# Two cached-attention blocks on one core: the wait for a pack's output weights moves to GpSimd, and the flag copy moves behind the last sum

## The chip, the core and the metric

The kernel runs on one core of a Trainium2 chip. A core has five instruction streams that run beside each other: TensorE (PE, matmuls; PEld is its weight load), VectorE (DVE), ScalarE (ACT), GpSimd (POOL) and SyncE (SP, which here only issues DMA transfers). Streams wait for each other through semaphores. The metric is the device time of one launch in microseconds (us); less is better.

## The reference

There are two independent blocks, A and B, of the same form; their results stand side by side in the output.

```python
# x [16, 64, 640], k_cache and v_cache [16, 32, 512, 128], wq [640, 4096], wo [4096, 640], all bf16
q = (x @ wq) -> [16, 32, 64, 128]
scores = einsum("bhqd,bhkd->bhqk", q, k_cache) * 128 ** -0.5
p = softmax(scores)
o = einsum("bhqk,bhkd->bhqd", p, v_cache)
return o -> [16, 64, 4096] @ wo
```

Nearly all bytes are the K and V caches: 2 blocks x 2 caches x 16 x 32 x 512 x 128 bf16 values.

## The kernel before, in words

**Packs.** The work is cut into 128 packs. A pack is four heads of a pair of batch rows, so its 2 x 64 queries fill 128 partitions. Four packs in a row (j = 0 to 3) make a group: 16 heads of one batch pair. Eight groups make a phase: one block and one half of its heads. There are four phases of 32 packs: A first half, A second half, B first half, B second half.

**What a pack does.** For pack n, in the names of the code and with the lines under which the profile shows them: QP (L684, PE) projects the queries, QE (L690, ACT) copies them out; KT (L698, DVE, two instructions) transposes the loaded K; S (L708, PE) makes the scores; EX (L737, ACT, four instructions, one for each head) takes the exponential and its sum; RC (L750, DVE, two instructions) inverts the sums; NM (L758, POOL, four instructions, heads 4n to 4n+3) multiplies P by them; TR (L770, PE) transposes P; TE (L850, DVE, two instructions, b = 0 and 1) copies transposed P out of PSUM; PV (L863, PE) multiplies by V; OE and ZO (L871, L875, ACT) copy the result out and clear PSUM; OP (L883, PE) multiplies by the pack's rows of wo and adds up over the four packs of a group in PSUM; OS (L893, L896, DVE) takes the sum out at the end of a group. At the start of a group XT, XE, XS and XC (L658, L664, L673) turn x around, and around the start of a phase WP (L652, POOL) lays out the next query weights.

**Loads.** SP issues all loads from one list: V (L642, L644; four pack slots), K (L631; six pack slots), x (L605), wq (L613) and wo (LDWO, L621). wo has four slots, one for each j, of 640 KB each. A slot is loaded once in a phase, for the phase's first group, and read by eight packs. In the list the load of wo for pack n stands behind V of pack n and K of pack n+3, and ahead of V of pack n+1. V of pack n waits until TR of pack n-3 is done.

**The order.** A planner (`build_plan`) gives every operation a due time, in packs, from the table `AT`: due time = pack + offset. Each engine's program is its operations sorted by due time, and each engine runs its program strictly in that order. From what operations read and write the planner finds which must wait for which, leaves out what an engine already knows through an earlier wait, and writes the rest as semaphore waits. For pack n the due times are: TE n+1.432 and n+1.47, PV n+1.701, OP n+2.387; NM of the next pack n+1.803 to n+2.187; TR of the next pack n+2.293. So between TE of pack n and OP of pack n, PE does PV of pack n, S of pack n+2 and TR of pack n+1, and TR of pack n+1 waits for the last NM of pack n+1.

**Where a wait may stand.** OP reads the wo slot, but does not wait for its load itself: a loop behind the planner's dependencies moves that wait to another operation that comes earlier and that PE waits for anyway. It moves two sorts: LDWO (the loads) and WZ (the clearing of two slots that two empty packs -2 and -1 read). The same loop puts the wait for a load of x (LDX) on the last NM of a pack, on POOL.

**The end.** The last pack (127) is done in two halves. OSH (L835, DVE, two instructions, due 127+1.75 and 127+1.8) adds each half of the last sum into the output tile, and SP stores each half (STH, L842, 80 KB). The kernel also checks that no sum left a safe range: FL1 (L908 to L915, DVE), FLM (L919, PE) and FLC (L923, DVE, due 127+1.77) leave a flag in SBUF. Each of the five streams waits for FLC, loads the flag into a register (L987) and branches (L988) over a second version of the program, which runs only where the flag says so. SP then waits for the stores (L529).

Of the kernel before, what the change touches and what calls it, by code (L numbers as in the profile page):

```python
# [20 lines left out]
class Cfg:  # L21
# [16 lines left out]
              RCZ=(0.475, 0.6), NMZ=(0.48, 0.49, 0.61, 0.62), TR=1.293, TE=(1.432, 1.47), PV=1.701, OE=(1.888, 2.013), ZO=2.221,  # L38
              OP=2.387, OS=2.576, LDWO=2.6, ST=2.8,
              TRH=(1.0, 1.05), TEH=(1.15, 1.2), TEX=1.2, PVH=(1.45, 1.46), OEH=(1.5, 1.55), OPY=(1.1, 1.57),  # L40
              OPZ=(1.65, 1.7), OSH=(1.75, 1.8), STH=(1.85, 1.9), FL1=1.3, FLM=1.68, FLC=1.77, WP0=-1.75,
              WP1=(-3.5, -2.55, -2.45, -1.5, -0.5, 0.5, 0.6, 1.5))


# [42 lines left out]
def build_plan(dims, cfg, general):  # L87
# [6 lines left out]
    N = NPH * PH  # L94
# [3 lines left out]
    at = {}  # L98

    def add(eng, kind, idx, ts, reads=(), writes=()):  # L100
        op = Op(eng, kind, idx, ts, reads, writes)
        ops.append(op)
        at[(kind, idx)] = op
        return op

    def add_output(n):
# [6 lines left out]
        if n == N - 1:  # L113
            for a in range(2):
# [5 lines left out]
                    [("B", 4), ("B", 5), ("xe", 0)] if a == 0 else [("SB", 2), ("SB", 3), ("xe", 1)])  # L120
                add("pe", "OPH", (n, a), n + AT["OPZ"][a], [("xe", 0), ("xe", 1), ("wo", j)], [("B", 6 + a)])
                add("dve", "OSH", (g, a), n + AT["OSH"][a], [("acc", g % NBP)], [("B", 6 + a), ("out_sb", a)])
# [47 lines left out]
    for ph in range(NPH):  # L170
        twp = [ph * PH + (AT["WP1"][i] if ph else i // 2 + AT["WP0"] + i % 2 * 0.001) for i in range(2 * NJ)]
        for kt in range(dims["KT"] if ph else 0):
            ready = twp[-1] - PH + 0.5 if ph > 1 else NJ - 1 + AT["WP0"] + 0.5
            op = add("sp", "LDWQ", (ph, kt), twp[0] - 0.5, [], [("ws", kt, j) for j in range(NJ)])
# [18 lines left out]
    for n in range(-2, N):  # L193
# [6 lines left out]
        for i in range(4):  # L200
            if i < 2 or n < cfg.KSPLIT:
                op = add("sp", "LDK", (n, i), n + AT["KT"][0] - 0.9, [], [("kn", n % cfg.NK)])
# [51 lines left out]

    for op in ops:
        if op.kind in ("OP", "OPH"):
            at[("TE", (op.idx, 1)) if op.kind == "OP" else ("TE", (op.idx[0], 1)) if op.idx[0] < N - 1 else ("TEH", 1)].deps += [d for d in op.deps if d.kind in ("LDWO", "WZ")]
            op.deps = [d for d in op.deps if d.kind not in ("LDWO", "WZ")]
        if op.kind == "XT" and op.idx > 0:
            at[("NM", 4 * (NJ * op.idx - NJ) + 3)].deps += [d for d in op.deps if d.kind == "LDX"]  # L260
            op.deps = [d for d in op.deps if d.kind != "LDX"]
        if op.kind == "QP" and op.idx > 0:
            op.deps = [d for d in op.deps if d.kind != "WP"]
# [238 lines left out]
def mha_kernel(nc, blocks, out, cfg=None):  # L502
# [20 lines left out]
    for general in (False, True):  # L523
        dims = dict(NPH=NPH, NBP=NBP, NJ=NJ, KT=KT, FIRST=lambda ph: ph % NSUB == 0,
                    FINAL=lambda ph: ph % NSUB == NSUB - 1)
        plans.append(build_plan(dims, cfg, general))
# [540 lines left out]
```

## Time and profile before

| | before |
|---|---|
| median of 3 runs | 738.27 us (737.86 to 738.68) |
| profiled execution, its own time | 737.86 us |
| span in that profile | 736.1 us |
| PE busy | 679.2 us (92%) |
| DVE / ACT / POOL busy | 526.9 / 533.2 / 416.5 us |
| read from HBM / rate over the span | 292.03 MB / 400 GB/s |

The span runs from the first to the last instruction of the program; the profiled execution's own time is 1.76 us longer. "Idle before, releaser" names what ended an engine's idle time. In the table of windows, DMA share is the summed time of packets over 16 engines' time, so it can be a little over 1. A landing time is the time from a transfer's issue until its semaphore says that it is done. "Chain" is the path followed back from the last instruction through whatever released each step.

### The profile page before, as it was taken

Reading aid. Unit: us, or ns where it says so; the run is one execution under the profiler, and the core shown is the slowest. Engines: PE = TensorE matmul, PEld = TensorE weight load, DVE = VectorE, ACT = ScalarE, POOL = GpSimd, SP = SyncE. Lnnn points to the kernel's source line nnn. Section 1 sums busy time; section 2 is a strip of 40 time slices with the busy share of each in tenths; the row PEclk is TensorE's granted clock in tenths of the full one; section 3 lists DMA queues with packets and bytes.
Section 4 is the critical chain, followed back from the end, with each engine's and each line's share of the span. In section 5 each row is a group of like instructions: output and inputs, shape, how many; then the busy total and the mean of one; then the engine's idle time right before and its main releaser. Section 6 shows DMA issues by size and latency. Waiting matters only on the chain.

```text
span 736.1 us, 61429 instructions
## 1 busy us (share of the span) xinstructions
PE 679.2 (92%) x28502; PEld 532.5 (72%) x28502; DVE 526.9 (72%) x819; ACT 533.2 (72%) x1574; POOL 416.5 (57%) x596
## 2 busy tenths in 40 slices
PE   3679999999989999999988999999998899999997
PEld 2457877877767777777766787777776678778785
DVE  7347877878767876867756777776676578788884
ACT  1348787877876887777865777777776687878874
POOL 3635656557864555454865565565577456555561
PEclk9889999999999999999998999999999999999999
DMA  8999999999999999999999999999999999999991
GB/s 325 393 392 411 415 415 414 414 416 413 416 400 410 417 417 416 415 419 416 416 412 400 416 414 414 414 414 413 416 416 405 404 418 417 415 419 416 417 400 45
DMA packets 76131, 295.06 MB, mean 401 GB/s; under 512 B 9536, under 2 KB 24512, under 8 KB 59712
## 3 DMA queue, kind: packets, MB, share of 16 engines
q1 hardware_dynamic: 73328, 291.90, 98.4%
q10 hardware_dynamic: 2768, 2.79, 1.2%
q8 instruction: 10, 0.16, 0.1%
q14 instruction: 25, 0.20, 0.1%
HBM read 292.03 MB, written 2.62 MB: 400 GB/s over the span
## 4 chain that ended last, share of the span: by engine, by line
PE 60%; DMA 27%; SPq 5%; DVE 3%; issue 2%; POOL 1%; ACT 0%; ACTq 0%
PE ps L863 14%; PE ps L883 13%; PE ps L684 12%; PE ps L708 12%; DMA wo_sb<-in_B_wo_dram 8%; PE ps L770 7%; DMA kn_ring<-in_B_k_cache_dram 5%; DMA kn_ring<-in_A_k_cache_dram 5%; DMA xn_ring<-in_B_x_dram 5%; SPq L631 3%; SPq L642 2%; DMA ws_sb<-in_A_wq_dram 2%; DMA wo_sb<-in_A_wo_dram 2%; DVE kt_ring L698 1%; DVE pT_sb L850 1%
## 5 line engine op out<-in xcount | busy, mean ns | idle before, releaser
L758 POOL TENSOR_SCALAR pn_ring<-pn_ring,recip 128x512 bf16<-128x512 bf16 x508 | 342.1, 692 | 244.9 <-DVE recip L750 238.5
L698 DVE STREAM_TRANSPOSE kt_ring<-kn_ring 128x1024 f32<-128x1024 f32 x256 | 302.4, 1220 | 65.9 <-DMA kn_ring<-in_B_k_cache_dram 35.7
L737 ACT ACTIVATE pn_ring<-ps 128x512 bf16<-128x512 f32 x512 | 296.4, 592 | 6.8 <-PE ps L708 6.8
L850 DVE COPY pT_sb<-ps 128x1024 bf16<-128x1024 bf16 x256 | 170.3, 676 | 103.5 <-PE ps L770 80.1
L863 PE MATMUL ps<-pT_sb,v_ring 32*128 32x64 bf16 x16448 | 162.1, 193 | 25.3 <-DVE pT_sb L850 12.7
L863 PEld LDWEIGHTS ps<-pT_sb,v_ring 32*128 32x128 bf16 x16448 | 147.5, 92 | 39.2 <-issue 28.7
L684 PE MATMUL ps<-xT_ring,wqp_sb 128*128 128x128 bf16 x2560 | 166.3, 221 | 7.5 <-POOL xT_ring L673 7.5
L684 PEld LDWEIGHTS ps<-xT_ring,wqp_sb 128*128 128x128 bf16 x2560 | 158.0, 114 | 14.0 <-issue 7.8
L883 PE MATMUL ps<-wo_sb,oT_sb 128*128 128x320 bf16 x1024 | 165.3, 305 | 0.0
L871 ACT ACTIVATE oT_sb<-ps 128x256 bf16<-128x256 f32 x257 | 84.7, 381 | 109.3 <-PE ps L863 109.3
L708 PE MATMUL ps<-kt_ring,qs_ring 32*64 32x512 bf16 x4096 | 140.6, 386 | 3.6 <-issue 3.6
L690 ACT ACTIVATE qs_ring<-ps 128x512 bf16<-128x512 f32 x128 | 76.4, 597 | 65.3 <-PE ps L684 62.6
L883 PEld LDWEIGHTS ps<-wo_sb,oT_sb 128*128 128x128 bf16 x1024 | 91.0, 99 | 37.9
L770 PEld LDWEIGHTS ps<-ident,pn_ring 64*128 64x128 bf16 x4096 | 68.8, 96 | 66.9 <-ACT oT_sb L871 48.0
L737 ACT ACTIVATION_READ_ACCUMULATOR pn_ring<-ps 128x1 f32 x512 | 105.3, 206 | 0.0
L770 PE MATMUL ps<-ident,pn_ring 64*128 64x64 bf16 x4096 | 83.8, 192 | 12.3 <-POOL pn_ring L758 4.5
L708 PEld LDWEIGHTS ps<-kt_ring,qs_ring 32*64 32x64 bf16 x4096 | 53.2, 104 | 33.2 <-issue 5.9
L750 DVE RECIPROCAL recip<-rowsum 128x2 f32<-128x2 f32 x256 | 41.0, 160 | 30.3 <-ACT pn_ring L737 24.6
L875 ACT ACTIVATE ps<-zeros 128x256 f32<-128x256 bf16 x128 | 49.5, 387 | 4.1
L652 POOL COPY wqp_sb<-ws_sb 128x1280 bf16<-128x1280 bf16 x32 | 39.5, 1253 | 18.3 <-DMA ws_sb<-in_A_wq_dram 15.1
L664 ACT ACTIVATE xe_sb<-ps 128x640 bf16<-128x640 bf16 x32 | 23.0, 717 | 3.6 <-PE ps L658 3.6
L673 POOL COPY xT_ring<-xe_sb 128x640 bf16<-128x640 bf16 x16 | 11.5, 716 | 21.9 <-PE ps L770 21.9
(42 smaller groups left out, 103.7 us busy)
## 6 DMA issues: line engine op xcount, KB each, us to landing
v_ring<-in_A_v_cache_dram SPq DMA_DIRECT2D x128, 512.0 KB, 12.9
kn_ring<-in_B_k_cache_dram SPq DMA_DIRECT2D x128, 512.0 KB, 14.0
v_ring<-in_B_v_cache_dram SPq DMA_DIRECT2D x128, 512.0 KB, 12.8
kn_ring<-in_A_k_cache_dram SPq DMA_DIRECT2D x112, 512.0 KB, 14.1
kn_ring<-in_A_k_cache_dram SPq DMA_DIRECT2D x32, 256.0 KB, 9.0
wo_sb<-in_A_wo_dram SPq DMA_DIRECT2D x8, 640.0 KB, 14.6
ws_sb<-in_B_wq_dram SPq DMA_DIRECT2D x10, 512.0 KB, 17.3
wo_sb<-in_B_wo_dram SPq DMA_DIRECT2D x8, 640.0 KB, 15.0
```

What stands on the lines that cost most here:

```text
L684: last = e.matmul(ps[:, 1, f * 128:(f + 1) * 128], w[:, kt, f, :], xT_ring[:, xs, kt, :], start=(kt == 0), stop=(kt == KT - 1))
L690: ins = e.activation(qs_ring[:, op.idx % NQ].rearrange("p f b q -> p (f b q)"), ps[:, 1, :], ACTF.Copy, scale=scale)
L698: ins = e.transpose(dst.rearrange("p c b (h l) -> p c h b l", h=8, l=2), src)
L708: last = e.matmul(ps[64 * b:64 * b + 64, i, :], qs_ring[rows, n % NQ, f, b, :], kt_ring[rows, n % NKT, :, f // 2, b, :, f % 2], start=(f = ...
L737: ins = e.activation(dst, src, ACTF.Exp, scale=1.0, accum_out=sum_of(h))
L758: ins = e.tensor_scalar(pn_view(h), pn_view(h), recip[:, h:h + 1], 1.0, ALU.mult, ALU.mult)
L770: last = e.transpose(pt_bank(b)[:, 64 * c:64 * c + 64], pn[rows, c, :], ident[rows, rows], tile_position=(64 * b, 0))
L850: ins = e.tensor_copy(pT_sb[:, b].rearrange("p t q -> p (t q)"), pt_bank(b))
L863: last = e.matmul(ps[:, 4 + i, 64 * b:64 * b + 64], v_ring[rows, n % NV, b, c, :], pT_sb[rows, b, c, :], start=(t == 0 and i < 2), stop=(t ...
L871: ins = e.activation(oT_sb[:, 2 * a:2 * a + 2, :], o_ps[:, 2 * a:2 * a + 2, :], ACTF.Copy)
L875: ins = e.activation(z_ps, zeros[:, :].unsqueeze(2).broadcast_to([128, 2, 128]), ACTF.Copy)
L883: last = e.matmul(out_ps[:, s, :], oT_sb[:, i, :], wo_sb[:, 4 * j + i, s * NH0:(s + 1) * NH0], start=(j == 0 and i == 0), stop=(j == NJ - ...
```

## The change

The wait for a load of wo (and for WZ) moves from the second TE of the same pack, on DVE, to the last NM of the next pack, on POOL: for OP of pack n that is NM of head 4n+7 (for the empty pack -2 it is NM -1, a clearing of a P slot). OP of the last two packs keeps its place (TE of pack 126, TEH of pack 127). The due time of FLC goes from 1.77 to 1.82, so that it stands behind both OSH on DVE instead of between them. No operation is added or removed.

```diff
-              OPZ=(1.65, 1.7), OSH=(1.75, 1.8), STH=(1.85, 1.9), FL1=1.3, FLM=1.68, FLC=1.77, WP0=-1.75,
+              OPZ=(1.65, 1.7), OSH=(1.75, 1.8), STH=(1.85, 1.9), FL1=1.3, FLM=1.68, FLC=1.82, WP0=-1.75,
...
     for op in ops:
         if op.kind in ("OP", "OPH"):
-            at[("TE", (op.idx, 1)) if op.kind == "OP" else ("TE", (op.idx[0], 1)) if op.idx[0] < N - 1 else ("TEH", 1)].deps += [d for d in op.deps if d.kind in ("LDWO", "WZ")]
+            at[("NM", 4 * op.idx + 7 if op.idx >= -1 else -1) if op.kind == "OP" else ("TE", (N - 2, 1)) if op.idx[0] < N - 1 else ("TEH", 1)].deps += [d for d in op.deps if d.kind in ("LDWO", "WZ")]
             op.deps = [d for d in op.deps if d.kind not in ("LDWO", "WZ")]
```

## The prediction

> **What bounds the kernel now.** I read the page first, which has PE busy for most of the span and the DMA engines busy in every slice but the first and the last; then busy time by 10 us windows, the waits, the timeline around a phase start and around the end, and last the chain. Four of the windows (the columns are the stretch and its length, PE, PEld, DVE, ACT and POOL busy, the granted clock, the DMA share and GB/s):
>
> ```profile
> 560.00:570.00 10.00, 6.69 (x315) 5.55 (x301) 6.20 (x9) 4.81 (x14) 5.28 (x8) 0.90 1.04 401
> 580.00:590.00 10.00, 7.04 (x380) 5.53 (x380) 6.67 (x10) 4.96 (x15) 4.07 (x6) 1.00 1.03 410
> 590.00:600.00 10.00, 10.00 (x447) 8.08 (x439) 8.12 (x14) 8.22 (x26) 5.38 (x8) 1.00 1.02 416
> 700.00:710.00 10.00, 10.00 (x440) 7.81 (x438) 7.83 (x12) 7.75 (x25) 5.88 (x10) 1.00 1.02 418
> ```
>
> Two limits lie almost on each other. The DMA engines are never idle while loads run: the DMA share stays above 1.00 and the rate near 416 GB/s, lower only where wo is loaded (401 to 410 at 560 to 590). PE, too, is full from 590 to the end. It idles at the phase starts, where four packs need 640 KB of wo each on top of their K and V. The waits on the tile of wo, its landing times, and two rows of the waits on POOL:
>
> ```profile
>   DVE pT_sb L850: 23.4, 12
> DMA to landing us min/median/max: 11.1/14.7/17.7
> ...
> POOL pn_ring L758 <- DMA xn_ring<-in_B_x_dram: 6.0, 6, 1.7
> PE ps L770 <- POOL pn_ring L758: 4.5, 6, 1.3
> ```
>
> TE (L850) waits for wo 12 times, four at each of three phase starts, 23.4 us in all. wo takes 11 to 18 us to land, with a full DMA queue ahead of it.
>
> **The change, part by part.** *1. The wait at a phase start.* The last phase starts at pack 96. The first, third and last of its four stalled copies, what follows the last on PE, and NM at the usual pace:
>
> ```profile
> 566.61 0.69 DVE L850 COPY pT_sb<-ps 128x1024 bf16<-128x1024 bf16 x1 [3.54 <-DMA wo_sb<-in_B_wo_dram]
> ...
> 580.35 0.69 DVE L850 COPY pT_sb<-ps 128x1024 bf16<-128x1024 bf16 x1 [2.01 <-DMA wo_sb<-in_B_wo_dram]
> ...
> 587.22 0.69 DVE L850 COPY pT_sb<-ps 128x1024 bf16<-128x1024 bf16 x1 [2.28 <-DMA wo_sb<-in_B_wo_dram]
> ...
> 588.05 1.21 PE L863 MATMUL ps<-pT_sb,v_ring 32*128 32x64 bf16 x128 [1.77 <-DVE pT_sb L850]
> ...
> 590.20 0.64 PE L770 MATMUL ps<-ident,pn_ring 64*128 64x64 bf16 x32
> ...
> 699.42 2.69 POOL L758 TENSOR_SCALAR pn_ring<-pn_ring,recip 128x512 bf16<-128x512 bf16 x4 [2.04 <-DVE recip L750]
> ```
>
> Today wo of pack 99 lands at 587.22; the copy, PV and S follow, and TR of pack 100 starts at 590.20, 2.98 us after the landing. With the wait on the last NM, copy, PV and S of pack 99 are done before the landing, and behind it stands one NM (four take 2.69 us, so 0.67 each) with about 0.1 us of semaphore: TR of pack 100 at 588.0. That is 2.2 us earlier. The same holds at the packs before it: each of the four transposes starts a landing plus 0.8, the first at 567.4 (566.61 + 0.8).
>
> What stands behind the waiting NM on POOL is NM of the next pack (its sums are not there yet), and once in a group XC; WP of the phase is all ahead of it. XC waits for the transpose just before it and takes as long as an OP, behind which PE comes to the QP that needs it: hidden, but with little to spare. On PE everything behind TR waits, but the first of it is OP, which needs that wo anyway. POOL's wait passes on almost whole: the waits for x that already stand on the same NM cost POOL 6.0 us and PE 4.5. Taking the wait off TE costs nothing; it only lets RC and KT, queued behind it on DVE, go earlier. SP issues the same list, and V of a later pack is let go by an earlier TR, so its issues come earlier or as now.
>
> *2. What is late next.* The landings stay where they are, since the DMA engines were never idle: an earlier issue only waits longer in the queue. So the 2.2 us are worth what K allows. In the stretch that K binds the chain shows the shortest way from a K landing to PV, by KT, both copies and OS:
>
> ```profile
> 275.39 18.48 DMA kn_ring<-in_A_k_cache_dram
> 293.89 1.85 DVE kt_ring L698 x2
> ...
> 297.50 0.73 DVE out_sb L896
> 298.37 1.21 PE ps L863 x128
> ...
> DVE kt_ring L698 <- DMA kn_ring<-in_B_k_cache_dram: 0.8, 4, 0.3
> ...
> 710.75 1.25 DVE L698 STREAM_TRANSPOSE kt_ring<-kn_ring 128x1024 f32<-128x1024 f32 x1
> 716.13 1.21 PE L863 MATMUL ps<-pT_sb,v_ring 32*128 32x64 bf16 x128
> ```
>
> Landing at 293.87 to PV at 298.37: 4.5 us. At the same place of a group near the end, KT at 710.75 to PV at 716.13 takes 5.4. From 680 to 717 KT waits for K four times, 0.8 us in all: K lands just as KT is ready for it, so 710.75 is a landing time too. PE can therefore be ahead by 5.4 - 4.5 = 0.9 us at the end, whatever it gained at 590. **Part 1 is worth -0.9 us.** At the two earlier phase starts the gain is 0: the stretch behind each ends in a wait for K. Ends: -2.2, if K does land earlier; 0, if PE falls back to where it is. The first load of wo (no waits there today) and WZ (a clearing done in the first 11 us, against an NM at 19) cost nothing.
>
> *3. The flag.* The end of the kernel:
>
> ```profile
> 731.34 0.14 DVE L923 CAST flag<-ps 1x1 int32<-1x1 f32 x1
> 731.46 1.01 SPq L842 DMA_DIRECT2D out_dram<-out_sb  x2
> 731.61 0.49 DVE L835 TENSOR_TENSOR out_sb<-acc,ps 128x320 bf16<-128x320 f32 x1
> ...
> L987 ACTq TENSOR_LOAD <-flag x1: 490/490/490, 731.5 to 731.5; - x1
> L987 SPq TENSOR_LOAD <-flag x1: 507/507/507, 732.5 to 732.5; - x1
> DMA to landing us min/median/max: 1.6/2.6/3.6
> ...
> SPq L529 <- DMA out_dram<-out_sb: 2.6, 1, 2.6
> ```
>
> The second OSH starts when PE is done, flag or not, so moving FLC behind it does not bring the store's issue forward. It makes the flag later: from 731.48 to 731.61 + 0.49 + 0.14, less 0.09 overlap as today, 732.15, so +0.67. SP reads the flag only after its second issue, at 732.5: no change there. The two stores have the same size, yet one lands in 1.6 us and the other in 3.6. The second (issued near 732.1, landed 735.7) sets the end. The DMA rows of three windows (731.4 to 733.05, 733.05 to 733.45, 733.45 to 735.8) show what is different:
>
> ```profile
> q1 hardware_dynamic: 166, 0.10, 19.0%
> ...
> q1 hardware_dynamic: 104, 0.06, 46.8%
> q14 instruction: 3, 0.02, 26.5%
> ...
> q1 hardware_dynamic: 18, 0.01, 4.1%
> q8 instruction: 1, 0.02, 2.6%
> q14 instruction: 1, 0.01, 0.8%
> ```
>
> 270 of the 288 store packets are through by 733.45. From 733.05 on the streams that have loaded the flag (731.5 + 0.5) and branched fetch code, five fetches in all, and 18 store packets are left over until behind them. With the flag 0.67 later the first fetch comes near 733.7, when a store without fetches is through: landing 1.6 us after issue, 733.7 instead of 735.7. **Part 3 is worth -2.0 us.** Ends: -2.0, and +0.7 if the fetches still meet the store and only come later.
>
> *Sum.* The profiled execution took 737.86, 0.41 under the median shown. 737.86 - 0.9 - 2.0 = 735.0; on the median, 738.27 - 2.9 = **735.4 us**.
>
> **A rule weighed against the trace.** PE needs 5.12 us for a pack (PV of pack 99 at 588.05, of pack 124 at 716.13), while wo lands every 6.87 (580.35 to 587.22): PE will idle for 1.75 us ahead of each of the last three transposes. Does the clock drop?
>
> ```profile
> 220.00:222.00 2.00, 0.22 (x4) 0.09 (x3) 0.84 (x3) 0.60 (x1) 0.33 (x1) 1.00 1.06 424
> 224.00:226.00 2.00, 2.00 (x57) 1.10 (x42) 0.19 (x1) 1.29 (x4) 0.00 (x0) 0.50 1.04 385
> 586.00:588.00 2.00, 0.28 (x6) 0.12 (x3) 0.79 (x3) 0.60 (x1) 0.39 (x1) 1.00 1.02 412
> 588.00:590.00 2.00, 1.95 (x160) 1.54 (x160) 2.00 (x2) 0.66 (x2) 1.36 (x2) 1.00 1.05 426
> 388.00:390.00 2.00, 1.77 (x128) 1.77 (x128) 2.00 (x4) 0.00 (x0) 2.00 (x4) 0.50 1.04 390
> 392.00:394.00 2.00, 2.00 (x37) 1.45 (x38) 0.76 (x2) 1.94 (x7) 0.14 (x1) 0.52 1.03 411
> ```
>
> After a gap of 1.8 us at 220 the granted clock was 0.50 at 224; after the same gap at 586 it stayed 1.00. The Trainium skill, "TensorE: Matmul & The Clock Gate" (Part 1: The HAM clock gate), says that the clock halves after an idle window of about 3.4 us. By that rule gaps of 1.75 us cost nothing, and the sum is as above; the row at 224 does not bear it out, so the drop stays a rival.
>
> **The rivals.**
> *A: the forecast*, 735.4.
> *B: the fetches meet the store again.* The store's last packets then finish as late as now; part 1 alone is left: 738.27 - 0.9 = 737.4. For it: the fetches follow the flag whenever it comes. Against it: the first store, with no fetch beside it, lands in 1.6 us.
> *C: PE's lead is lost*, because K binds more tightly than the one place I measured: 738.27 - 2.0 = 736.3. For it: KT already waits four times before 717.
> *D: the branch sets the end.* If a stream cannot go on until its code is there, the end moves with the flag, +0.67, and 738.27 - 0.9 + 0.67 = 738.0. Against it: SP's last wait, 2.6 us, is put down to the store. The Trainium skill, "Runtime: NRT & Kernel Launch" (Instruction fetch mechanics), says that a taken branch out of the window has to fetch before it goes on; the wait for the store says that here something else was later.
> *E: slower, by the clock.* The three gaps of 1.75 us before the transposes of packs 98 to 100 each drop the clock for the 6 us of 388 to 394, 3 us lost each; the gap that follows takes back 1.75 of the first two. Lost: 1.25 + 1.25 + 3.0 = 5.5, less the 2.2 gained: 3.3 late at 590, and PE has no idle time after that to catch up. 738.27 + 3.3 - 2.0 = 739.6. It makes the kernel slower once a drop costs over 4.2 us in all (2.2 and 2.0). Against it: most gaps of this size left the clock alone.
>
> **How the numbers follow.** 0.2%, about 1.5 us, is what a measurement of this kernel can tell from no change. Chances: A 0.48, B 0.18, C 0.11, D 0.11, E 0.12. A and C are faster by more than 0.2% (0.59), B and D lie within it (0.29), E is taken as slower (0.12), since a drop of the full length lies at its edge. The range goes from 734.4 (part 1 worth 1.9, near its end) up to 738.1, behind D; E and a little below are left out. A's own range is 734.4 to 736.2.
>
> **What would show it.** In the waits, TE's wait for wo is gone and NM (L758) waits for wo 12 times, some 20 us; PE's TR (L770) waits for NM by about as much; KT's waits for K between 592 and 717 grow from about 1 us to several. TR of pack 100 starts about 0.8 us after the last wo lands. Both stores land in under 2 us, and no code is fetched before the store's packets are through. The clock stays at 1.00 behind 575. I am wrong if the second store still takes 3 us or more, if the DMA share falls below 1.00 before 710, or if K lands at other times.

## The result and the profile after

The changed kernel takes 734.95 us (median of 6 runs, 734.22 to 736.06), the kernel before 738.07 us in the runs beside it. The ratio is 0.996, with a 95% interval of 0.9946 to 0.9975: faster by 3.0 us (1.8 to 4.0). The forecast was 735.4 us, 2.9 us faster. The profiled execution took 735.05 us, with a span of 733.3.

The windows of the changed kernel that answer to those shown of before (columns: stretch, its length, PE, PEld, DVE, ACT and POOL busy, granted clock, DMA share, GB/s):

```profile
560.00:570.00 10.00, 9.55 (x372) 7.46 (x358) 7.98 (x13) 7.96 (x24) 6.40 (x9) 1.00 1.04 402
580.00:590.00 10.00, 7.32 (x270) 5.89 (x271) 5.99 (x11) 5.87 (x21) 3.49 (x6) 1.00 1.03 408
590.00:600.00 10.00, 10.00 (x441) 7.87 (x439) 7.38 (x13) 7.78 (x22) 6.01 (x9) 1.00 1.02 415
700.00:710.00 10.00, 10.00 (x442) 7.93 (x440) 7.93 (x12) 7.96 (x24) 6.04 (x10) 1.00 1.02 417
```

The transfers run as before: share above 1.00, 402 to 408 GB/s while wo is loaded, 415 to 417 after. PE is busier at the start of the last phase (9.55 instead of 6.69 us in 560 to 570), at full clock. The waits of the whole span, and three of the stretch from 592 to 712:

```profile
PE ps L770 <- POOL pn_ring L758: 19.5, 14, 2.7
POOL pn_ring L758 <- DMA wo_sb<-in_B_wo_dram: 15.8, 7, 3.4
POOL pn_ring L758 <- DMA xn_ring<-in_B_x_dram: 8.8, 7, 2.9
POOL pn_ring L758 <- DMA wo_sb<-in_A_wo_dram: 5.0, 3, 2.5
...
DVE kt_ring L698 <- DMA kn_ring<-in_B_k_cache_dram: 20.0, 24, 1.8
PE ps L863 <- DVE out_sb L896: 0.4, 1, 0.4
PE ps L863 <- DVE pT_sb L850: 0.2, 1, 0.2
```

TE no longer waits for wo. NM does, 20.8 us in 10 places, and TR waits for NM 19.5 us instead of 4.5. Behind 592, KT waits for K 24 times, 20.0 us; before, it waited there for less than 1 us. The last landing of wo and what follows it, then the place where PE waits longest behind K, and KT of pack 126 and PV of pack 124 near the end:

```profile
586.95 0.69 POOL L758 TENSOR_SCALAR pn_ring<-pn_ring,recip 128x512 bf16<-128x512 bf16 x1 [2.46 <-DMA wo_sb<-in_B_wo_dram]
...
587.79 0.64 PE L770 MATMUL ps<-ident,pn_ring 64*128 64x64 bf16 x32 [1.76 <-POOL pn_ring L758]
...
628.58 2.37 DVE L698 STREAM_TRANSPOSE kt_ring<-kn_ring 128x1024 f32<-128x1024 f32 x2 [1.39 <-DMA kn_ring<-in_B_k_cache_dram]
...
633.06 1.21 PE L863 MATMUL ps<-pT_sb,v_ring 32*128 32x64 bf16 x128 [0.36 <-DVE out_sb L896]
...
638.09 1.56 PE L863 MATMUL ps<-pT_sb,v_ring 32*128 32x64 bf16 x128
...
710.50 2.37 DVE L698 STREAM_TRANSPOSE kt_ring<-kn_ring 128x1024 f32<-128x1024 f32 x2 [0.54 <-DMA kn_ring<-in_B_k_cache_dram]
715.40 1.22 PE L863 MATMUL ps<-pT_sb,v_ring 32*128 32x64 bf16 x128
```

TR of pack 100 starts 0.84 us after the landing, 2.4 us earlier than before. At pack 108 PV waits for OS, which stands behind KT, which waits for K: 628.58 to 633.06 is 4.48 us, the shortest way from K to PV that the kernel before had shown in its K-bound stretch. Besides these 0.36 us PE waits only 0.17 us behind K, at PV of pack 107, where TE stands behind a KT that waited for K. The PV of pack 109 (638.09) takes 1.56 us instead of 1.22, with no wait named; more on it below. And the end, in the timeline, the landing times of the two stores, SP's last wait, and the DMA rows of the stretches 729.9 to 732.9 and 732.9 to 733.32:

```profile
730.66 1.01 SPq L842 DMA_DIRECT2D out_dram<-out_sb  x2
730.82 0.49 DVE L835 TENSOR_TENSOR out_sb<-acc,ps 128x320 bf16<-128x320 f32 x1 [0.19 <-PE ps L827]
731.22 0.14 DVE L923 CAST flag<-ps 1x1 int32<-1x1 f32 x1
...
DMA to landing us min/median/max: 1.6/1.6/1.6
SPq L529 <- DMA out_dram<-out_sb: 0.6, 1, 0.6
...
q1 hardware_dynamic: 288, 0.16, 17.8%
...
q14 instruction: 3, 0.02, 20.6%
q8 instruction: 1, 0.02, 18.2%
```

All 288 packets of the two stores are through before the first fetch of code. Both stores land in 1.6 us, and SP waits 0.6 us for them instead of 2.6. The second OSH starts at 730.82 (731.61 before): of the 2.8 us by which the span is shorter, 0.8 lie ahead of it and 2.0 behind.

### The profile page after: what moved, and what is told of

Read it like the earlier page. It is cut to its first block, busy times and chain, and to the rows that moved or that the text cites. A ratio compares the mean times of both kernels' runs of the same rounds, so it can differ in the third digit from the quotient of the medians.

```text
span 733.3 us, 61431 instructions
## 1 busy us (share of the span) xinstructions
PE 680.6 (93%) x28502; PEld 533.9 (73%) x28502; DVE 523.9 (71%) x819; ACT 532.9 (73%) x1574; POOL 416.6 (57%) x596
## 4 chain that ended last, share of the span: by engine, by line
PE 55%; DMA 29%; SPq 7%; DVE 3%; POOL 2%; issue 2%; ACT 0%; ACTq 0%; POOLq 0%
PE ps L863 13%; PE ps L883 12%; PE ps L684 11%; PE ps L708 10%; DMA kn_ring<-in_B_k_cache_dram 7%; DMA kn_ring<-in_A_k_cache_dram 7%; PE ps L770 7%; DMA xn_ring<-in_B_x_dram 6%; DMA wo_sb<-in_B_wo_dram 4%; SPq L631 4%; SPq L642 3%; DMA ws_sb<-in_A_wq_dram 2%; DMA wo_sb<-in_A_wo_dram 2%; DVE kt_ring L698 2%; POOL pn_ring L758 1%
## 5 line engine op out<-in xcount | busy, mean ns | idle before, releaser
L708 PE MATMUL ps<-kt_ring,qs_ring 32*64 32x512 bf16 x4096 | 139.0, 382 | 2.8 <-issue 2.8
L770 PE MATMUL ps<-ident,pn_ring 64*128 64x64 bf16 x4096 | 83.8, 192 | 26.3 <-POOL pn_ring L758 19.5
```

Source lines behind the costliest of these rows:

```text
L708: last = e.matmul(ps[64 * b:64 * b + 64, i, :], qs_ring[rows, n % NQ, f, b, :], kt_ring[rows, n % NKT, :, f // 2, b, :, f % 2], start=(f = ...
L770: last = e.transpose(pt_bank(b)[:, 64 * c:64 * c + 64], pn[rows, c, :], ident[rows, rows], tile_position=(64 * b, 0))
```

## The experiments

Rival theories stood against each other for each part. For the flag: code fetched behind the branch gets between the packets of the second store; or the flag has no part in it. For wo: 2.2 us are won at the last phase start and K's landings cut them; or the whole lead reaches the end; or each phase start gives a share. All ratios are to the kernel before, run on the same chip beside it.

**Each part alone.** `flag_only` keeps the wait on TE; `wait_only` keeps FLC between the two OSH.

```diff
 # flag_only
-              ... FLC=1.77, ...
+              ... FLC=1.82, ...
 # wait_only
-            at[("TE", (op.idx, 1)) if op.kind == "OP" else ...
+            at[("NM", 4 * op.idx + 7 if op.idx >= -1 else -1) if op.kind == "OP" else ...
```

> Only FLC goes behind the second OSH; the wait for wo stays on TE. My theory (code that the streams fetch behind the branch gets between the packets of the second store): that store lands in about 1.6 us instead of 3.6, the end comes 2.0 us earlier, ratio 0.9973; PE's last matmul stays where it is. Rival (the flag has no part in it, the wait for wo brings all of it): second store still 3.6 us, ratio 1.000.

> Only the wait for wo moves to the last NM of the next pack; FLC stays between the two OSH. My theory (2.2 us won at the last phase start, cut to under 1 us by K's landings): the last PV of pack 124 about 0.8 us earlier, the second store still 3.6 us to land, ratio 0.9989. Rival (the lead of 2.2 us reaches the end): ratio 0.9970. Rival (no gain, DMA bound throughout): ratio 1.000.

Measured: the flag alone 0.9971 (0.9962 to 0.998), the wait alone 0.9989 (0.9979 to 0.9999); together they had given 0.996. The last timeline rows and SP's last wait, of the flag alone:

```profile
730.86 1.01 SPq L842 DMA_DIRECT2D out_dram<-out_sb  x2
731.02 0.49 DVE L835 TENSOR_TENSOR out_sb<-acc,ps 128x320 bf16<-128x320 f32 x1 [0.19 <-PE ps L827]
731.42 0.14 DVE L923 CAST flag<-ps 1x1 int32<-1x1 f32 x1
...
SPq L529 <- DMA out_dram<-out_sb: 0.6, 1, 0.6
```

With the flag alone the store wait is 0.6 us; in the profile of the wait alone the same row reads 2.7 us, and the flag copy stands at 730.82, ahead of the second OSH. In that trace 18 of the 288 store packets start behind the first fetch (from 732.83 on), like the 18 left over behind 733.45 in the kernel before; with the flag alone none does. PV of pack 124 in the wait alone comes 0.5 us earlier, by its distance from the last landing of wo (587.14 to 715.55, before 587.22 to 716.13), against the 0.8 expected. So the 2 us behind the second OSH belong to the flag and the rest to the wait, and they add up.

**Is it where the flag is copied, or when the branch is taken?** `flag_held` leaves the order on DVE as it was and only holds four of the five streams back.

```diff
             e.wait_ge(sems[0][("s_flc_dve",)], 1)
+            if eng != "sp":
+                e.wait_ge(sems[0][("s_osh_dve",)], 2)
```

> As before, FLC between the two OSH and the wait for wo on TE; but the four streams other than SP wait for both OSH before they load the flag, so that only their branch, and the code fetched behind it, comes 0.6 to 0.7 us later. Theory (the fetches get between the second store's packets): second store lands in 1.6 us, ratio 0.997, as with FLC moved. Rival (where FLC stands on DVE is what counts): second store 3.6 us, ratio 1.000.

Measured: 0.9972 (0.9955 to 0.9988), the same as with FLC moved. The rows of the end:

```profile
730.68 0.14 DVE L923 CAST flag<-ps 1x1 int32<-1x1 f32 x1
730.79 1.00 SPq L842 DMA_DIRECT2D out_dram<-out_sb  x2
730.95 0.49 DVE L835 TENSOR_TENSOR out_sb<-acc,ps 128x320 bf16<-128x320 f32 x1
...
L989 ACTq TENSOR_LOAD <-flag x1: 482/482/482, 731.5 to 731.5; - x1
...
SPq L529 <- DMA out_dram<-out_sb: 0.6, 1, 0.6
```

The flag is copied 0.27 us before the second OSH starts, as before, but the streams load it at 731.5, 0.8 us after the copy; the store wait is 0.6. It is the time of the branches that counts; the place of FLC on DVE makes no difference that these runs can tell. That the fetches are what the branches bring rests on the rows of packets: the store is late in the two traces where its packets meet the fetches (before, and the wait alone) and on time in the three where they do not (the whole change, the flag alone, the branches held back).

**Which phase starts count?** The wait moves only for packs 96 and later, or only for those below 96; each once with the flag as before, and once with the flag late.

```diff
 # last phase only
-            at[("TE", (op.idx, 1)) if op.kind == "OP" else ...
+            at[(("NM", 4 * op.idx + 7) if op.idx >= 96 else ("TE", (op.idx, 1))) if op.kind == "OP" else ...
 # early phases only
+            at[(("TE", (op.idx, 1)) if op.idx >= 96 else ("NM", 4 * op.idx + 7 if op.idx >= -1 else -1)) if op.kind == "OP" else ...
```

> The wait for wo moves only for packs 96 and later (the last phase start); in the two phase starts before, it stays on TE; FLC as before. My theory (only the last phase start has no K wait behind it that takes the gain back): the same as moving all of them, the end 0.8 us earlier, ratio 0.9989. Rival (each phase start gives a third): 0.3 us, ratio 0.9996.

> The wait for wo moves only for the packs below 96 (the second and third phase start); the last phase start keeps it on TE; FLC as before. My theory: nothing at the end, ratio 1.000, and in the stretch before pack 96 KT waits for K as before, with TR of pack 96 within 0.3 us of its old time. Rival (each phase start gives a third): 0.5 us, ratio 0.9993.

> FLC behind both OSH, the wait for wo on the last NM only for packs 96 and later. Theory (only the last phase start counts): the same as the whole change, ratio 0.996; KT to PV of pack 110 near 4.5 us (before 5.5). Rival (the earlier phase starts carry a part of it, as 0.9998 for the last phase alone suggests): ratio 0.997.

> FLC behind both OSH, the wait for wo on the last NM only for packs below 96. Theory: the same as the flag alone, ratio 0.997; KT to PV of pack 110 stays at 5.5 us. Rival (the wait at the early phase starts costs something, as 1.0014 for them alone suggests): ratio 0.9985.

| where the wait moves | flag as before | flag late |
|---|---|---|
| nowhere | 1 | 0.9971 (0.9962 to 0.998) |
| last phase start | 0.9998 (0.9989 to 1.0007) | 0.9963 (0.9948 to 0.9978) |
| the two before it | 1.0014 (1.0002 to 1.0025) | 0.9976 (0.996 to 0.9993) |
| all | 0.9989 (0.9979 to 0.9999) | 0.996 (0.9946 to 0.9975) |

With the flag late the picture is the expected one: the last phase start gives what the whole change gives, the two before it nothing that can be told. With the flag as before the last phase alone missed its expectation (0.9998 for 0.9989, at the end of the interval), and the early phases alone came out slower, which was not expected and did not come back with the flag late. The differences are of the size of the intervals; whether the early phase starts cost a few tenths of a us stays open. Of the finer expectations, KT of pack 110 to PV of pack 108 took 4.86 us with the last phase start and the late flag (forecast near 4.5, before 5.52) and 5.50 with the early ones (forecast 5.5). With the early ones and the flag as before, TR of pack 96 started 5.23 us ahead of the next landing of wo (559.93 to 565.16), before 4.91 (561.70 to 566.61): 0.3 us that the wait for wo then takes back.

The profile of the last phase start alone with the late flag shows what a drop of the clock does here. The last landing of wo, the windows of the last gap, PE's timeline there and PV of packs 100 and 124:

```profile
586.04 0.69 POOL L758 TENSOR_SCALAR pn_ring<-pn_ring,recip 128x512 bf16<-128x512 bf16 x1 [2.45 <-DMA wo_sb<-in_B_wo_dram]
...
586.00:588.00 2.00, 1.12 (x34) 0.95 (x35) 0.78 (x2) 1.61 (x6) 0.69 (x1) 0.76 1.02 414
588.00:590.00 2.00, 2.00 (x10) 1.19 (x9) 1.20 (x3) 0.00 (x0) 0.70 (x2) 0.50 1.06 430
...
586.88 0.93 PE L770 MATMUL ps<-ident,pn_ring 64*128 64x64 bf16 x32 [1.76 <-POOL pn_ring L758]
587.74 2.31 PE L883 MATMUL ps<-wo_sb,oT_sb 128*128 128x320 bf16 x8
...
591.64 1.22 PE L863 MATMUL ps<-pT_sb,v_ring 32*128 32x64 bf16 x128
...
714.57 1.22 PE L863 MATMUL ps<-pT_sb,v_ring 32*128 32x64 bf16 x128
```

The gap of 1.76 us ahead of TR is the one of the changed kernel, but here the granted clock fell to 0.50 behind it: OP took 2.31 us instead of 1.26. This is what rival E describes, once instead of three times. From the landing to PV of pack 100 it takes 5.60 us, against 4.00 in the changed kernel (586.95 to 590.95) and 6.14 before (587.22 to 593.36): most of the lead is gone at once. Yet at PV of pack 124 the two kernels are level, 128.53 us behind the landing here and 128.45 in the changed kernel (before 128.91), and this execution took 734.35 us, where the changed kernel's took 735.05. So in this execution the drop cost nothing that can be seen at the end, and it does not explain the miss with the flag as before.

**Is it the wait's place on DVE, or what comes between wo and TR?** `late_flag_first_nm` takes the wait off DVE too, but puts three more NM between wo and TR.

```diff
-            at[("TE", (op.idx, 1)) if op.kind == "OP" else ...
+            at[("NM", 4 * op.idx + 4 if op.idx >= -1 else -1) if op.kind == "OP" else ...
```

> FLC behind both OSH, the wait for wo on the first NM of the next pack (head 4n+4) instead of the last, so that four NM instead of one come between wo's landing and TR. Theory: TR of pack 100 starts 2.8 us behind the last landing of wo (0.8 with the last NM, 3.0 before), so only 0.2 us are won, and the ratio is that of the flag alone, 0.997. Rival (taking the wait off DVE is what helps, wherever it goes): ratio 0.996.

Measured: 0.9969 (0.9954 to 0.9985), the flag's share and no more. The last landing:

```profile
586.15 2.69 POOL L758 TENSOR_SCALAR pn_ring<-pn_ring,recip 128x512 bf16<-128x512 bf16 x4 [4.20 <-DMA wo_sb<-in_B_wo_dram]
...
588.99 0.64 PE L770 MATMUL ps<-ident,pn_ring 64*128 64x64 bf16 x32 [1.79 <-POOL pn_ring L758]
```

TR starts 2.84 us behind the landing (2.98 before, 0.84 with the last NM). Freeing DVE by itself is worth nothing that these runs can tell.

**Do the loads cut the lead?** The same pair of kernels, wait on TE and wait on the last NM, both with the late flag, and with a quarter of the loads left out from pack 100 on.

```diff
             n, b = op.idx
-            if n < 0:
+            if n < 0 or n >= 100 and b:
                 return None, None
```

> FLC behind both OSH, the wait for wo on TE as before. Left out: the second V load (b = 1) of packs 100 and later, so PV reads what lay in that half slot; the DMA engines get a quarter less to do from the last phase start on, and K lands earlier than PE needs it. Both theories: PE was the limit there before, so the end stays where FLC alone put it, ratio 0.997; no KT wait for K behind 600.

> The whole change (the wait for wo on the last NM, FLC behind both OSH), with the same V loads left out. My theory (of the 2.2 us won at 590, K's landings let only 0.7 to 0.9 through): with K early the whole 2.2 us reach the end, ratio 0.994, which is 0.003 under the kernel beside it. Rival (something else than K cuts the lead, the clock or PE's own order): the difference stays at 0.001, as with the loads whole.

Measured: 0.997 (0.9958 to 0.9982) with the wait on TE, 0.9932 (0.9918 to 0.9946) with the wait on the last NM. The difference is 0.0038, against 0.0011 with the loads whole. In neither does KT wait for K behind 600. The last release by wo and the second OSH, first with the wait on TE, then on NM:

```profile
586.55 0.69 DVE L850 COPY pT_sb<-ps 128x1024 bf16<-128x1024 bf16 x1 [2.26 <-DMA wo_sb<-in_B_wo_dram]
...
730.83 0.49 DVE L835 TENSOR_TENSOR out_sb<-acc,ps 128x320 bf16<-128x320 f32 x1 [0.19 <-PE ps L827]
```

```profile
587.79 0.69 POOL L758 TENSOR_SCALAR pn_ring<-pn_ring,recip 128x512 bf16<-128x512 bf16 x1 [2.46 <-DMA wo_sb<-in_B_wo_dram]
...
729.65 0.49 DVE L835 TENSOR_TENSOR out_sb<-acc,ps 128x320 bf16<-128x320 f32 x1 [0.19 <-PE ps L827]
```

From the landing to the second OSH it takes 144.28 us with the wait on TE and 141.86 with the wait on NM: 2.4 us. The whole of what was won at TR (2.1 by its distance from the landing) reaches the end once there is less to load; the other 0.27 us arise behind PV of pack 126 (6.39 us to the second OSH in one trace, 6.12 in the other). With the loads whole, the same way takes 144.39 us before (587.22 to 731.61) and 143.87 after (586.95 to 730.82): 0.5 us. And the kernel with the wait on TE gained nothing from a quarter less to load (0.997 with or without), so PE was its limit there. The edit relieves all loads, K's and the others' (DMA share 0.90 from 600 to 700 with the wait on TE, 1.02 in the changed kernel), so it shows that the loads take the lead, not which of them.

No version with all its loads beat the changed kernel.

## Why the prediction was right, point by point

- *The wait's new place wins 2.2 us at 590.* Right: TR of pack 100 at a landing plus 0.84 (forecast 0.8), 2.4 us earlier, 0.27 of it because the landing came earlier in this execution. With the first NM instead of the last the gain was gone, so it is the work between wo and TR that counts.
- *The landings stay where they are.* Right: wo of pack 99 landed at 586.95 instead of 587.22, and the DMA share stayed above 1.00 to 710.
- *K lets 0.9 us through.* Right in part. That the loads cut the lead is shown: with less to load it arrives whole, and the run whose clock dropped was level with the changed kernel at pack 124. That K's landing does it the profile shows for a third. PE's lead over the kernel before was 2.41 us at PV of pack 100 (590.95 and 593.36), 1.26 at pack 108 (633.06 and 634.32) and 0.73 at pack 124 (715.40 and 716.13); 0.27 of it is the earlier landing. Of the 1.68 us lost, 0.53 are the two waits behind K, at packs 107 and 108. Most of the rest went inside PV: in 7 of the 25 packs from 100 to 124 it takes 1.35 to 1.56 us instead of 1.22 (in 2 before, in none with thinned loads). What PE waits for there the profile does not say; it is not the landing of V, which by the trace came at least 0.85 us before each of these PV began. At the end PE was not at the limit of 4.5 us from K to PV: from 710.50, where K lands, to PV of pack 124 at 715.40 are 4.90 us. In the trace of the wait alone it was (711.08 to 715.55, 4.47 us). The 0.9 was worked out at one place near the end. It lies within what the runs of the wait alone gave, 0.8 us (0.1 to 1.5); the traces, from the last landing of wo to the second OSH, gave 0.5. That the size came so near is partly luck.
- *The two earlier phase starts give nothing.* Borne out with the late flag (0.9976 beside 0.9971 for the flag alone), not settled with the flag as before.
- *The flag's move is worth 2.0 us, by the code fetches.* Right in size (0.9971, 2.1 us) and cause: holding the branches back, with the flag copied as before, gave 0.9972.
- *Rivals.* B and D fall with the store's 1.6 us and the end that came earlier with a later flag. C falls, though not by much: the wait alone gave 0.9989, with an interval that ends at 0.9999, and 0.5 us of the lead reached the second OSH in the traces. E did not decide, but a drop behind a short gap is real: one run showed the clock halved behind a 1.76 us gap. There it cost nothing that can be seen at the end. PE did idle 1.73 to 1.76 us ahead of each of the last three transposes, as forecast, and in the changed kernel the clock stayed at 1.00 behind them. The Trainium skill, "TensorE: Matmul & The Clock Gate" (Part 1: The HAM clock gate), ties the drop to an idle window of about 3.4 us; the granted clock of 0.50 behind the gap of 1.76 us in that run does not agree with it.
- *NM waits 12 times, some 20 us; KT "several".* 10 times, 20.8 us; KT 20.0 us.

## What to carry to other kernels

A wait belongs on the last thing that the consumer's engine waits for anyway, and what it is worth is the work that used to stand between the landing and that point; then ask at once what the next landing allows, since with busy DMA engines a lead of over 2 us shrank to 0.5 here. A branch at the end of a kernel can cost more than its own time: here the code fetched behind it held up the last packets of a store and cost 2 us, so let the store's packets go first. Parts of one change are best run alone: the line that looked like tidying, the flag's due time, brought most of the gain.

## What the runs showed of the hardware that I had not expected

A store of 80 KB lands in 1.6 us alone and in 3.6 us when a handful of code fetches (8 KB on one queue, 16 KB on another) run between its packets. The same gap of 1.76 us on PE left the granted clock at 1.00 in one execution and halved it in another. With the DMA engines full, PV takes 0.13 to 0.34 us longer in some packs with no wait named; with a quarter less to load it does so in none.
